# Scores of both heads of an early pair issued in turns into two PSUM banks, in one step

## The chip, the cores and the metric

The kernel runs on one core of a Trainium2 chip. The metric is the device time of one execution in microseconds, taken over several runs. The trace is that of one profiled execution, and its times count from the start of its span.

## The reference

An attention with a memory, then two feed-forward layers over all 2304 tokens. B = 4 batches, H = 8 heads, S = 576 tokens, D = 64; the model's width is 512, the inner width of the layers 2048.

```python
scores = scale * np.matmul(q, k.transpose(0, 1, 3, 2))        # per head 576 x 576, causal
a = exp(scores - rowmax); a /= a.sum(-1) + 1e-09
local = np.matmul(a, v)
q_p = phi(q)                                                  # elu(q) + 1
mem_out = (q_p @ M_prev) / (q_p @ z_prev + 1e-6)
attn = g * mem_out + (1 - g) * local                          # g = sigmoid(beta) per head
x = attn, heads side by side: 2304 x 512
h = x @ w_in;  g = max(h, 0) + log1p(exp(-|h|));  x = g @ w_out
h = x @ w_in2; g = h if h > 0 else exp(h) - 1;    out = g @ w_out2
```

## The kernel before

**Staging.** Each batch's attention is cut into part A, the first 256 tokens (two query tiles, 0 and 1, of 128 rows), and part B, the other 320. The layers run over five chunks of tokens: chunk 0 is part A of batches 0 and 1, chunk 1 part A of batches 2 and 3, and chunks 2 to 4 hold the parts B. So the parts A of batches 0 and 1 come first, at the start of the program (`chain`), and every other attention part is side work: `sides()` is a generator that is advanced while a chunk's layer runs. The layer's loop (`ffn`) has 16 f steps of 12 matmuls (L572 to L574, four k of three each, into a bank "h"), an activation (L548 to L551 in layer 0: Abs, Exp, Ln, then a DVE step), a cast and a difference (L576, L577), and then 16 output steps of 12 matmuls (L588 to L590). All products are in full precision from two or three passes of a split operand; a plain fp32 matmul shows as two records in the trace.

**What sets the order.** `TUNE["order"]` lists chunk and layer with shares: (1.9, 0.0) says that 1.9 steps of side work and 0.0 weight conversions are owed for every f step, and the second bracket says so for every output step. `conv` says after which step of the start the conversion of weights begins, and in what rhythm. Within that, a scheduler orders the instructions of each engine by priority and by its own estimate of times; so an instruction's place in the program text is not its place in an engine's queue. Each engine works through its queue in order.

**Part A in the plain path.** A pair p is two heads; head h of a pair lies in partitions 64h to 64h + 63. One score matmul multiplies 128 query columns of one head by 128 (tile 0) or 256 (tile 1) key columns, over 64 rows of the array (`product`, L294). `bank(n)` gives a 2 KB bank from "h" (four buffers, shared with the layers) for batches 0 and 1, and from pss (three buffers, shared with the transposes "tp") for batches 2 and 3. `scores(n, (0, 1))` writes tile 0 of one head into a bank, lets DVE reduce it with the mask into `sph` and `neg` (L320), lets ACT take exp (L326), and then does tile 1 in the same bank. `normalise` scales the rows of sph, `group` transposes them (L361) and copies them to `pt`, `gather_pair` multiplies with v and the memory (L392, L395), and an ACT cast and a DVE difference write the layer's operand x (L142, L143). `feature(p)` computes phi and its norm: ACT L241 and L242 (reading `ar`, loaded by POOL at L192 to L198), DVE L243 to L252; `feature_t` transposes it (L261).

Early in the program PE's order has, among others, one behind the other: h_553 of 128 columns (an odd head), h_426 of 256 columns (an odd head), h_590 of 128 columns (an even head).

**Weights.** `convert` builds the two-part weights (L506, L508, L97) and stores them to DRAM scratch; SP loads them again for later chunks (L532).

Of the kernel before, what the change touches and what calls it, by code (L numbers as in the profile page):

```python
# [10 lines left out]
ACTF = mybir.ActivationFunctionType  # L11
ALU = mybir.AluOpType
AX = mybir.AxisListType
I32 = mybir.dt.int32
# [21 lines left out]
WIDTH = [sum(n for _, _, n in c) for c in CHUNKS]  # L36
SLOT = (0, 1, 2, 0, 1)
TUNE = dict(
    st='q', pri=(200, 200), conv=(4, 2, 14), inw=4, ahead=(3, 3, 0), pads=0, plain=(0, 1, 2, 3),
    hi='ssss ssss', lo='v', sc='vv vvv ssv', pt='s ssv', eva='sv',  # L40


    order=((0, 0, (1.9, 0.0), (0.8, 0.2)), (1, 0, (0.2, 0.2), (0.8, 0.6)), (0, 1, (1.1, 0.0), (1.2, 0.0)), (1, 1, (1.1, 0.0), (1.5, 0.0)), (2, 0, (0.4, 0.0), (1.2, 0.0)), (2, 1, (0.8, 0.0), (1.2, 0.0)), (3, 0, (0.4, 0.0), (1.2, 0.0)), (3, 1, (0.8, 0.0), (1.0, 0.0)), (4, 0, (0.0, 0.0), (0.0, 0.0)), (4, 1, (0.0, 0.0), (0.0, 0.0))),
)


# [12 lines left out]
def kernel(  # L59
# [85 lines left out]
    def attention(b, part, pool, early=None):  # L145
# [159 lines left out]
        def scores(n, todo):  # L305
            P = sph[n % 2]
            neg = d["neg", n]
            ps = None
            for i in todo:
                w_ = width(i)  # L310
                pieces = ((0, w_),) if i < 4 else ((0, S // 2), (S // 2, S // 2))
                for k, (k0, kn) in enumerate(pieces):
                    if first:
                        ps = ps if i else bank(n)
                        s = ps[:, poff(0, i):poff(0, i) + kn]
                    else:
                        s = bank(0)[:, :kn]
                    product(n, i, s, k0, kn)
                    mk0 = 512 - 128 * i + k0
                    ve.tensor_tensor_reduce(  # L320
                        out=P[:, poff(n, i) + k0:poff(n, i) + k0 + kn], in0=s, in1=mask[:, mk0:mk0 + kn],
                        scale=-0.125, scalar=3.0e38 if k == 0 else neg[:, 5:6], op0=ALU.add, op1=ALU.min,
                        accum_out=neg[:, 5:6] if i == 4 and k == 0 else neg[:, i:i + 1],
                    )
                Pi = P[:, poff(n, i):poff(n, i) + w_]
                se.activation(Pi, Pi, ACTF.Exp, scale=-1.0, bias=neg[:, i:i + 1], accum_out=sums(n, i))  # L326

        def scale(n):
            P = sph[n % 2]
# [90 lines left out]
        feature(0)  # L420
        prep_v(0)
        yield
        for n in range(H):
            p, hh = divmod(n, 2)
            start(n)
            if not plain and n + 1 < H:
                prep_qk(n + 1)
            if first:
                if hh == 0:
                    feature_t(p)  # L430
                scores(n, (0, 1))
                if hh and p + 2 < NP:
                    load_kq(p + 2)
                yield
                normalise(n)
                if hh == 0 and n:
                    group(n - 2, d["pt", n - 2][0], ((1, 0), (0, 0), (1, 1)))
                    group(n - 1, d["pt", n - 1][0], ((1, 0), (0, 0), (1, 1)))
                    yield
                    gather_pair(n - 2)  # L440
                    if p + 2 < NP:
                        load_rest(p + 2)
                if hh == 0 and p + 1 < NP:
                    feature(p + 1)
                d["pt", n] = targets(n)
                if n + 1 < H:
                    prep_v(n + 1)
                yield
                continue
            scores(n, (2,))  # L450
            yield
            if n:
# [46 lines left out]
    def convert(src, key, w=None):  # L499
        wr = tri.tile([128, 4, 128], F32, name="wr", tag="wr")  # L500
        if wide:
            w64 = tri.tile([128, 4, 128, 2], I32, name="w64", tag="big")
            nc.sync.dma_start(w64.rearrange("p k n t -> p (k n t)"), src.bitcast(I32))
            low, high = w64[:, :, :, 0], w64[:, :, :, 1]
            wi = wr.bitcast(I32)
            se.activation(wr, high.bitcast(F32), ACTF.Prelu, scale=2.0 ** -112, alpha=-(2.0 ** 32))  # L506
            ve.tensor_scalar(wi, wi, 3, None, ALU.logical_shift_left)
            ve.scalar_tensor_tensor(wi, low, 29, wi, ALU.logical_shift_right, ALU.bitwise_or)  # L508
        else:
            nc.sync.dma_start(wr.rearrange("p k n -> p (k n)"), src)  # L510
        if w is None:
            w = w64.rearrange("p k n t -> p (k n t)").rearrange("p (s k n) -> p s k n", s=2, k=4).bitcast(F32R)
        hi, lo = w[:, 0], w[:, 1]
        copy(E[T["hi"].split()["o" in key][int(key[0])]], hi, wr)
        E[T["lo"]].tensor_sub(lo, wr, f32(hi))
        scratch[key] = dram.tile([128, 2, 4, 128], F32, name=f"s_{key}", tag=f"s_{key}")
        E[T['st']].dma_start(scratch[key], f32(w))
# [109 lines left out]
    def chain(parts, ahead):  # L627

        parts, active = list(parts), []
        while parts or active:  # L630
            if parts and (not active or len(active) == 1 and active[0][2] <= ahead):
                b, part, pool, early = parts.pop(0)
                active.append([(b, part), attention(b, part, pool, early), 21 if part == "A" else 43])
            for a in list(active):
                a[2] -= 1
                if next(a[1], a) is a:
# [118 lines left out]
```

## Time and profile before

| | |
|---|---|
| time, median of 3 runs | 1084.99 us (1078.2 to 1086.96) |
| profiled execution: span | 1077.9 us |
| profiled execution: own time | the page gives no time beside the span |
| PE busy | 1043.4 us, 97% of the span |
| DVE busy, ACT busy | 684.7 us (64%), 670.5 us (62%) |
| POOL busy | 90.5 us (8%) |
| DMA moved | 251.65 MB, 233 GB/s |

PE is TensorE, DVE VectorE, ACT ScalarE, POOL GpSimd, SP SyncE; PEld is the loading of weights into TensorE. A row of the timeline gives a start, a duration, the engine, the line, what is written and read, and in brackets the idle time ahead with what ended it. Matmuls overlap, so the time that one takes of PE is the distance to the next one's start, not its duration. PEclk is the granted clock as a share of 2.4 GHz.

### The profile page before, as it was taken

To read this page: it belongs to the slowest core of one execution; us is meant where nothing else is said; L and a number is where in the kernel's file an instruction comes from. 1 tells how busy PE (TensorE), PEld (TensorE's weight loads), DVE (VectorE), ACT (ScalarE), POOL (GpSimd) and SP (SyncE) were. 2 spreads that over 40 slices of the span, in tenths; PEclk is the share of its full clock that TensorE was granted. 3 is DMA by queue.
4 is the path that set the end of the run, shared out by engine and by line. 5 is a ranking of instruction groups with operands and counts; after the bars stand their busy time and mean duration, and the time that the engine had idled before them with its cause. 6 is when DMAs were issued, how large, how long until landed. Compare 5 with 4: busy or idle time off the path is not lost.

```text
span 1077.9 us, 15779 instructions
## 1 busy us (share of the span) xinstructions
PE 1043.4 (97%) x5328; PEld 906.1 (84%) x5328; DVE 684.7 (64%) x1698; ACT 670.5 (62%) x1458; POOL 90.5 (8%) x173
## 2 busy tenths in 40 slices
PE   6799999989999999999999999999999999999998
PEld 3456676667888888888889998999999999999998
DVE  6966787666567998798557756875575271150540
ACT  5858886588558987576659945654796251480330
POOL 5222331000000000000000000000000000000000
PEclk9789999989999999999999999999999999999999
DMA  8891588887875788755765655666655477877775
GB/s 264 312 332 50 185 288 299 291 303 283 293 273 204 248 277 302 277 197 164 231 219 192 219 201 194 225 225 204 219 176 173 159 254 247 253 233 234 230 234 175
DMA packets 73120, 251.65 MB, mean 233 GB/s; under 512 B 10320, under 2 KB 14928, under 8 KB 73040
## 3 DMA queue, kind: packets, MB, share of 16 engines
q1 hardware_dynamic: 64432, 216.56, 59.2%
q0 software_dynamic: 8608, 34.09, 10.1%
q8 instruction: 42, 0.69, 0.3%
q14 instruction: 38, 0.31, 0.1%
HBM read 212.34 MB, written 38.27 MB: 233 GB/s over the span
## 4 chain that ended last, share of the span: by engine, by line
PE 82%; DMA 7%; DVE 5%; ACT 3%; issue 1%; SPq 0%; POOL 0%; DVEq 0%; ACTq 0%
PE h L588 12%; PE h L589 12%; PE h L590 12%; PE h L572 11%; PE h L573 10%; PE h L574 10%; PE tp L361 5%; DMA s_1i<-w 3%; PE o L376 2%; DMA w<-in_w2i 2%; PE s L298 2%; DMA w<-in_w1i 2%; PE h L298 1%; PE s L294 1%; PE o L377 1%
## 5 line engine op out<-in xcount | busy, mean ns | idle before, releaser
L572 PE MATMUL h<-x,w 128*128 128x512 f32 (+2 forms) x640 | 238.8, 379 | 10.7 <-ACT x L142 3.8
L573 PE MATMUL h<-x,w 128*128 128x512 f32 (+2 forms) x640 | 240.2, 375 | 0.0
L574 PE MATMUL h<-x,w 128*128 128x512 f32 (+2 forms) x640 | 240.1, 375 | 0.0
L588 PE MATMUL h<-g,w 128*128 128x512 f32 (+2 forms) x640 | 238.2, 373 | 0.2 <-DVE neg L320 0.2
L589 PE MATMUL h<-g,w 128*128 128x512 f32 (+2 forms) x640 | 237.2, 371 | 0.0
L590 PE MATMUL h<-g,w 128*128 128x512 f32 (+2 forms) x640 | 237.0, 371 | 0.0
L572 PEld LDWEIGHTS h<-x,w 128*128 128x128 f32 x640 | 120.7, 189 | 27.7 <-ACT x L142 4.5
L573 PEld LDWEIGHTS h<-x,w 128*128 128x128 f32 x640 | 121.4, 190 | 13.4 <-issue 1.5
L574 PEld LDWEIGHTS h<-x,w 128*128 128x128 f32 x640 | 121.4, 190 | 13.4 <-issue 0.3
L588 PEld LDWEIGHTS h<-g,w 128*128 128x128 f32 x640 | 120.2, 188 | 12.9 <-issue 0.7
L590 PEld LDWEIGHTS h<-g,w 128*128 128x128 f32 x640 | 120.2, 188 | 12.1 <-issue 1.0
L589 PEld LDWEIGHTS h<-g,w 128*128 128x128 f32 x640 | 120.3, 188 | 11.8 <-DVE sph L336 0.4
L577 DVE TENSOR_TENSOR g<-t,g 128x512 fp32r<-128x512 f32 (+2 forms) x160 | 100.9, 634 | 34.1 <-ACT g L576 32.7
L326 ACT ACTIVATE sph<-sph,neg 128x576 f32<-128x576 f32 (+2 forms) x160 | 96.2, 602 | 38.3 <-DVE neg L320 37.8
L576 ACT CAST g<-t 128x512 fp32r<-128x512 f32 (+2 forms) x160 | 91.3, 573 | 23.5 <-DVE t L559 19.2
L551 DVE SCALAR_TENSOR_TENSOR t<-h,t 128x512 f32<-128x512 f32 (+2 forms) x80 | 50.7, 636 | 61.2 <-ACT t L550 60.8
L367 DVE TENSOR_TENSOR ptb<-tp,ptb 128x512 fp32r<-128x512 f32 (+2 forms) x96 | 53.3, 575 | 39.0 <-ACT ptb L366 38.7
L320 DVE CUSTOM_DVE_ANT_0 sph<-s,mask 128x128 f32<-128x128 f32 (+4 forms) x80 | 38.4, 483 | 59.6 <-PE s L298 37.6
L366 ACT CAST ptb<-tp 128x512 fp32r<-128x512 f32 (+2 forms) x96 | 45.0, 498 | 47.6 <-PE tp L361 47.1
L361 PE MATMUL tp<-ident,sph 128*128 128x128 f32 x480 | 71.6, 282 | 0.4 <-DVE sph L336 0.4
L361 PEld LDWEIGHTS tp<-ident,sph 128*128 128x128 f32 x480 | 60.3, 146 | 7.7 <-DVE sph L336 1.0
L506 ACT ACTIVATE wr<-w 128x512 f32<-128x512 f32 x64 | 42.7, 667 | 33.0 <-DMA w<-in_w2i 14.1
(112 smaller groups left out, 1517.9 us busy)
## 6 DMA issues: line engine op xcount, KB each, us to landing
w<-s_1i SPq DMA_DIRECT2D x79, 512.0 KB, 3.8
w<-s_0i SPq DMA_DIRECT2D x64, 512.0 KB, 4.3
w<-s_0o SPq DMA_DIRECT2D x64, 512.0 KB, 3.9
w<-s_1o SPq DMA_DIRECT2D x64, 512.0 KB, 4.2
qk<-in_qk POOLq DMA_DIRECT2D x32, 480.0 KB, 5.0
w<-in_w1i SPq DMA_DIRECT2D x16, 512.0 KB, 5.7
s_0i<-w SPq DMA_DIRECT2D x16, 512.0 KB, 5.6
w<-in_w1o SPq DMA_DIRECT2D x16, 512.0 KB, 4.7
```

The costliest lines, as they stand in the source:

```text
L326: se.activation(Pi, Pi, ACTF.Exp, scale=-1.0, bias=neg[:, i:i + 1], accum_out=sums(n, i))
L361: te.transpose(pt[:, c:c + 128], P[:, poff(n, i) + 128 * j:poff(n, i) + 128 * j + 128], ident)
L367: ve.tensor_sub(dst[:, 1, :c], pt[:, :c], f32(dst)[:, 0, :c])
L551: ve.scalar_tensor_tensor(t, h, 0.0, t, ALU.max, ALU.add)
L572: te.matmul(h[:, :N], hi[:, k, :], xk[:, 0, :N], start=k == 0, stop=False)
L573: te.matmul(h[:, :N], hi[:, k, :], xk[:, 1, :N], start=False, stop=False)
L574: te.matmul(h[:, :N], lo[:, k, :], xk[:, 0, :N], start=False, stop=k == KD - 1)
L576: se.copy(g[:, 0, :N], t[:, :N])
L577: ve.tensor_sub(g[:, 1, :N], t[:, :N], f32(g)[:, 0, :N])
L588: te.matmul(h[:, :N], hi[:, k, :], gs[f][:, 0, :N], start=f == 0, stop=False)
L589: te.matmul(h[:, :N], hi[:, k, :], gs[f][:, 1, :N], start=False, stop=False)
L590: te.matmul(h[:, :N], lo[:, k, :], gs[f][:, 0, :N], start=False, stop=f == KF - 1)
```

## The change

One generator step now treats both heads of a pair. `scores_pair(n)` takes two banks, one for each head, issues tile 1 of both heads and then tile 0 of both heads, and then, head by head, the DVE reduction and the ACT exp of tile 1 and of tile 0. The loop over heads becomes a loop over pairs for the parts A. A part A takes 17 steps in place of 21. The shares of chunk 0, layer 0, are lowered from 1.9 and 0.8 to 1.6 and 0.6, and the first conversion comes after step 3 in place of 4. The w64 tile is also allocated where weights aren't wide.

```diff
--- before.py
+++ after.py
@@ -36,11 +36,11 @@
 WIDTH = [sum(n for _, _, n in c) for c in CHUNKS]
 SLOT = (0, 1, 2, 0, 1)
 TUNE = dict(
-    st='q', pri=(200, 200), conv=(4, 2, 14), inw=4, ahead=(3, 3, 0), pads=0, plain=(0, 1, 2, 3),
+    st='q', pri=(200, 200), conv=(3, 2, 14), inw=4, ahead=(3, 3, 0), pads=0, plain=(0, 1, 2, 3),
     hi='ssss ssss', lo='v', sc='vv vvv ssv', pt='s ssv', eva='sv',
 
 
-    order=((0, 0, (1.9, 0.0), (0.8, 0.2)), (1, 0, (0.2, 0.2), (0.8, 0.6)), (0, 1, (1.1, 0.0), (1.2, 0.0)), (1, 1, (1.1, 0.0), (1.5, 0.0)), (2, 0, (0.4, 0.0), (1.2, 0.0)), (2, 1, (0.8, 0.0), (1.2, 0.0)), (3, 0, (0.4, 0.0), (1.2, 0.0)), (3, 1, (0.8, 0.0), (1.0, 0.0)), (4, 0, (0.0, 0.0), (0.0, 0.0)), (4, 1, (0.0, 0.0), (0.0, 0.0))),
+    order=((0, 0, (1.6, 0.0), (0.6, 0.2)), (1, 0, (0.2, 0.2), (0.8, 0.6)), (0, 1, (1.1, 0.0), (1.2, 0.0)), (1, 1, (1.1, 0.0), (1.5, 0.0)), (2, 0, (0.4, 0.0), (1.2, 0.0)), (2, 1, (0.8, 0.0), (1.2, 0.0)), (3, 0, (0.4, 0.0), (1.2, 0.0)), (3, 1, (0.8, 0.0), (1.0, 0.0)), (4, 0, (0.0, 0.0), (0.0, 0.0)), (4, 1, (0.0, 0.0), (0.0, 0.0))),
 )
 
 
@@ -305,16 +305,11 @@
         def scores(n, todo):
             P = sph[n % 2]
             neg = d["neg", n]
-            ps = None
             for i in todo:
                 w_ = width(i)
                 pieces = ((0, w_),) if i < 4 else ((0, S // 2), (S // 2, S // 2))
                 for k, (k0, kn) in enumerate(pieces):
-                    if first:
-                        ps = ps if i else bank(n)
-                        s = ps[:, poff(0, i):poff(0, i) + kn]
-                    else:
-                        s = bank(0)[:, :kn]
+                    s = bank(0)[:, :kn]
                     product(n, i, s, k0, kn)
                     mk0 = 512 - 128 * i + k0
                     ve.tensor_tensor_reduce(
@@ -324,6 +319,23 @@
                     )
                 Pi = P[:, poff(n, i):poff(n, i) + w_]
                 se.activation(Pi, Pi, ACTF.Exp, scale=-1.0, bias=neg[:, i:i + 1], accum_out=sums(n, i))
+
+        def scores_pair(n):
+            ps = [bank(n), bank(n + 1)]
+            for i in (1, 0):
+                w_, at = width(i), poff(0, i)
+                for h in range(2):
+                    product(n + h, i, ps[h][:, at:at + w_], 0, w_)
+            for h in range(2):
+                P, neg = sph[h], d["neg", n + h]
+                for i in (1, 0):
+                    w_, at, to = width(i), poff(0, i), poff(n, i)
+                    ve.tensor_tensor_reduce(
+                        out=P[:, to:to + w_], in0=ps[h][:, at:at + w_], in1=mask[:, 512 - 128 * i:512 - 128 * i + w_],
+                        scale=-0.125, scalar=3.0e38, op0=ALU.add, op1=ALU.min, accum_out=neg[:, i:i + 1],
+                    )
+                    Pi = P[:, to:to + w_]
+                    se.activation(Pi, Pi, ACTF.Exp, scale=-1.0, bias=neg[:, i:i + 1], accum_out=sums(n + h, i))
 
         def scale(n):
             P = sph[n % 2]
@@ -420,33 +432,36 @@
         feature(0)
         prep_v(0)
         yield
-        for n in range(H):
+        for p in range(NP if first else 0):
+            n = 2 * p
+            start(n)
+            start(n + 1)
+            feature_t(p)
+            scores_pair(n)
+            if p + 2 < NP:
+                load_kq(p + 2)
+            yield
+            if p:
+                group(n - 2, d["pt", n - 2][0], ((1, 0), (0, 0), (1, 1)))
+                group(n - 1, d["pt", n - 1][0], ((1, 0), (0, 0), (1, 1)))
+                yield
+                gather_pair(n - 2)
+                if p + 2 < NP:
+                    load_rest(p + 2)
+            if p + 1 < NP:
+                feature(p + 1)
+            yield
+            normalise(n + 1)
+            for m in (n, n + 1):
+                d["pt", m] = targets(m)
+                if m + 1 < H:
+                    prep_v(m + 1)
+            yield
+        for n in range(0 if first else H):
             p, hh = divmod(n, 2)
             start(n)
             if not plain and n + 1 < H:
                 prep_qk(n + 1)
-            if first:
...
             scores(n, (2,))
             yield
             if n:
@@ -507,6 +522,7 @@
             ve.tensor_scalar(wi, wi, 3, None, ALU.logical_shift_left)
             ve.scalar_tensor_tensor(wi, low, 29, wi, ALU.logical_shift_right, ALU.bitwise_or)
         else:
+            w64 = tri.tile([128, 4, 128, 2], I32, name="w64", tag="big")
             nc.sync.dma_start(wr.rearrange("p k n -> p (k n)"), src)
         if w is None:
             w = w64.rearrange("p k n t -> p (k n t)").rearrange("p (s k n) -> p s k n", s=2, k=4).bitcast(F32R)
@@ -630,7 +646,7 @@
         while parts or active:
             if parts and (not active or len(active) == 1 and active[0][2] <= ahead):
                 b, part, pool, early = parts.pop(0)
-                active.append([(b, part), attention(b, part, pool, early), 21 if part == "A" else 43])
+                active.append([(b, part), attention(b, part, pool, early), 17 if part == "A" else 43])
             for a in list(active):
                 a[2] -= 1
                 if next(a[1], a) is a:
```

Inserted lines shift the numbers: L320, L548 to L551, L572 and L588 to L590 of before are L333, L564 to L567, L588 and L604 to L606 of the change; L392 and L395 are L404 and L407.

PE's queue at the first pair of batch 2 (s_908 and s_948, then s_909 and s_910, are the two heads' score banks; h is a layer bank). Before:

```order
L294 MATMUL s_908<-kq_845 128x128 [waits DMASW3_49,DMASW2_49]
L294 MATMUL s_948<-kq_845 128x128 [waits DMASW5_49,DMASW4_49]
L261 MATMUL tp_990<-ident_89,e_915 128x128 [waits DVE_49,Activation_49]
...
L572 MATMUL h_1115<-x0_0_96,w_404 128x512 [waits DVE_49]
...
L574 MATMUL h_1115<-x0_3_99,w_404 128x512
L294 MATMUL s_908<-kq_845 128x256 [waits DVE_49]
L294 MATMUL s_948<-kq_845 128x256 [waits DVE_49]
L572 MATMUL h_1166<-x0_0_96,w_433 128x512 [waits DVE_49]
```

And now:

```order
L261 MATMUL tp_904<-ident_89,e_870 128x128
L294 MATMUL s_909<-kq_845 128x256 [waits DMASW3_49,DMASW2_49]
L294 MATMUL s_910<-kq_845 128x256 [waits DMASW5_49,DMASW4_49,PE_49]
L294 MATMUL s_909<-kq_845 128x128
L294 MATMUL s_910<-kq_845 128x128
L588 MATMUL h_1123<-x0_0_96,w_456 128x512 [waits DVE_49]
L589 MATMUL h_1123<-x0_0_96,w_456 128x512
```

The two matmuls of a head, which stood 18 rows apart with a wait for DVE ahead of the second, now follow each other, in turns with those of the other head.

ACT's queue at the first layer's first two f steps (t_821 and t_880 are their activations, x0_3 the last operand of chunk 0, e and ar belong to `feature` of batch 2's first pairs). Before:

```order
L142 CAST x0_3_99<-o_803 128x256 [waits PE_49]
L548 ACTIVATE t_821<-h_823 128x512 [waits PE_49]
L548 ACTIVATE t_880<-h_882 128x512 [waits PE_49]
L549 ACTIVATE t_821<-t_821 128x512 [waits Activation_49]
L549 ACTIVATE t_880<-t_880 128x512 [waits Activation_49]
L550 ACTIVATE t_821<-t_821,ones_91 128x512 [waits Activation_49]
L241 ACTIVATE e_870<-ar_850 128x256 [waits DMASW4_49,DMASW6_49,DMASW3_49,DMASW7_49,DMASW2_49,DMASW0_49]
...
L550 ACTIVATE t_880<-t_880,ones_91 128x512 [waits Activation_49]
L242 ACTIVATE ar_850<-ar_850,ones_91 128x256 [waits Activation_49]
```

And now:

```order
L142 CAST x0_3_99<-o_803 128x256 [waits PE_49]
L564 ACTIVATE t_821<-h_823 128x512 [waits PE_49]
L241 ACTIVATE e_870<-ar_850 128x256 [waits DMASW4_49,DMASW3_49,DMASW6_49,DMASW2_49,DMASW7_49,DMASW0_49,Activation_49]
L241 ACTIVATE e_928<-ar_860 128x256 [waits DMASW2_49]
L564 ACTIVATE t_880<-h_882 128x512 [waits PE_49]
L565 ACTIVATE t_821<-t_821 128x512 [waits Activation_49]
L242 ACTIVATE ar_850<-ar_850,ones_91 128x256 [waits Activation_49]
L242 ACTIVATE ar_860<-ar_860,ones_91 128x256 [waits DMASW7_49,DMASW0_49,Activation_49]
L565 ACTIVATE t_880<-t_880 128x512 [waits Activation_49]
```

The two L241 moved ahead of the second f's first activation, and the two L242 ahead of its second.

PE's queue where chunk 1 begins (x1_2 and x1_3 are operands of chunk 1, o_2135 is the last gather of batch 3, g and h_2012 belong to chunk 0's output steps). Before:

```order
L574 MATMUL h_2255<-x1_1_101,w_2251 128x512
L572 MATMUL h_2186<-x1_2_102,w_2182 128x512 [waits Activation_49]
L572 MATMUL h_2209<-x1_2_102,w_2205 128x512
L572 MATMUL h_2232<-x1_2_102,w_2228 128x512
...
L392 MATMUL o_2135<-phi_1895,ar_1571 64x256 [waits DVE_49]
L392 MATMUL o_2135<-phi_1895,ar_1571 64x256
L573 MATMUL h_2186<-x1_2_102,w_2182 128x512
...
L395 MATMUL o_2135<-pt_2066,ar_1571 64x128
L572 MATMUL h_2186<-x1_3_103,w_2182 128x512 [waits Activation_49]
L572 MATMUL h_2209<-x1_3_103,w_2205 128x512
```

And now:

```order
L404 MATMUL o_2135<-phi_1872,ar_1552 64x256 [waits DMASW5_49,DVE_49]
L404 MATMUL o_2135<-phi_1872,ar_1552 64x256
L407 MATMUL o_2135<-pt_2042,ar_1552 64x256 [waits DMASW4_49,Activation_49]
...
L407 MATMUL o_2135<-pt_2043,ar_1552 64x128
L606 MATMUL h_2012<-g_1122,w_2044 128x512
L604 MATMUL h_2012<-g_1172,w_2044 128x512
...
L606 MATMUL h_2012<-g_1579,w_2110 128x512
L385 MATMUL o_2800<-phi_2568,ms_2176 128x320 [waits DVE_49]
L588 MATMUL h_2186<-x1_0_100,w_2182 128x512 [waits DMAHW1_49]
L589 MATMUL h_2186<-x1_0_100,w_2182 128x512
...
L588 MATMUL h_2186<-x1_3_103,w_2182 128x512 [waits Activation_49]
```

Before, all of chunk 0's output matmuls were through, and four f steps of chunk 1 were begun operand by operand ahead of the last gather; now 28 output matmuls stand behind that gather, and chunk 1's f steps follow whole.

## Rows read from the trace of the kernel before

**Rows 1.** The page, part 1: busy time, share of the span, instructions.
```profile
PE 1043.4 (97%) x5328; PEld 906.1 (84%) x5328; DVE 684.7 (64%) x1698; ACT 670.5 (62%) x1458; POOL 90.5 (8%) x173
```

**Rows 2.** Busy time by window: PE, PEld, DVE, ACT, POOL, granted clock, DMA share, GB/s.
```profile
40.00:60.00 20.00, 16.56 (x67) 10.42 (x68) 19.55 (x70) 15.89 (x43) 4.04 (x8) 0.59 0.96 349
80.00:100.00 20.00, 17.82 (x76) 12.75 (x74) 12.73 (x38) 16.46 (x39) 7.29 (x14) 0.91 0.24 68
100.00:120.00 20.00, 20.00 (x89) 13.61 (x89) 13.31 (x46) 17.06 (x40) 4.43 (x8) 1.00 0.21 65
200.00:220.00 20.00, 17.58 (x86) 11.41 (x86) 15.29 (x46) 12.39 (x33) 2.20 (x5) 1.00 0.66 225
220.00:240.00 20.00, 17.22 (x64) 13.35 (x63) 13.54 (x26) 16.86 (x31) 1.07 (x2) 0.83 0.89 313
```

**Rows 3.** PE's waits, 0 to 300 us: total, times, longest.
```profile
PE h L572 <- ACT x L142: 3.8, 3, 2.1
...
PE h L294 <- DVE neg L320: 0.3, 1, 0.3
```

**Rows 4.** Timeline of PE, 96 to 114 us: start, duration, instruction.
```profile
96.07 0.39 PE L573 MATMUL h<-x,w 128*128 128x512 f32 x1
96.30 0.39 PE L574 MATMUL h<-x,w 128*128 128x512 f32 x1
96.62 0.70 PE L294 MATMUL s<-kq 64*128 64x256 f32 x4
97.25 0.50 PE L572 MATMUL h<-x,w 128*128 128x512 f32 x1
97.59 0.39 PE L573 MATMUL h<-x,w 128*128 128x512 f32 x1
...
107.85 0.48 PE L294 MATMUL s<-kq 64*128 64x128 f32 x2
108.26 0.65 PE L395 MATMUL o<-pt,ar 128*64 128x256 f32 x2
...
113.17 0.70 PE L294 MATMUL s<-kq 64*128 64x256 f32 x2
113.80 0.50 PE L574 MATMUL h<-x,w 128*128 128x512 f32 x1
```

**Rows 5.** Timeline of PE, what ran between 21.81 and 22.04 us.
```profile
21.80 0.59 PE L294 MATMUL h<-kq 64*128 64x128 f32 x2
```

**Rows 6.** Timeline of PE at the second chunk's start.
```profile
219.53 1.19 PE L572 MATMUL h<-x,w 128*128 128x512 f32 x4 [2.15 <-ACT x L142]
...
226.78 0.47 PE L572 MATMUL h<-x,w 128*128 128x512 f32 x1 [2.78 <-DVE g L577]
```

**Rows 7.** Timeline of all engines, 77 to 86 us, down to e's first steps.
```profile
79.34 0.71 POOL L194 DMA_DIRECT2D ar<-in_vm  x1
...
81.22 1.09 ACT L548 ACTIVATE t<-h 128x512 f32<-128x512 f32 x2 [3.07 <-PE h L574]
...
82.19 1.15 ACT L549 ACTIVATE t<-t 128x512 f32<-128x512 f32 x2
...
83.23 0.72 ACT L550 ACTIVATE t<-t,ones 128x512 f32<-128x512 f32 x1
83.84 0.72 ACT L241 ACTIVATE e<-ar 128x256 f32<-128x256 f32 x2
...
83.98 0.69 DVE L551 SCALAR_TENSOR_TENSOR t<-h,t 128x512 f32<-128x512 f32 x1 [5.38 <-ACT t L550]
...
84.73 0.79 PE L572 MATMUL h<-x,w 128*128 128x512 f32 x1 [2.14 <-DVE t L551]
...
85.07 0.90 ACT L242 ACTIVATE ar<-ar,ones 128x256 f32<-128x256 f32 x2
...
85.81 0.75 DVE L243 SCALAR_TENSOR_TENSOR e<-e,ar 128x256 f32<-128x256 f32 x2
```

**Rows 8.** Tile ar, 60 to 215 us: time from a load's issue to landing.
```profile
DMA to landing us min/median/max: 2.1/3.4/6.8
```

More of the change, by code (lines that the diff above doesn't have):

```diff
@@ L427, in attention @@
                 prep_qk(n + 1)
-            if first:
[L429 to L449, printed above, removed]
             scores(n, (2,))
```

## The prediction

> **What bounds the kernel now.** The page's first part comes first: PE is busy 97% of the span [rows 1], so time leaves the span only if PE gets less to do or waits less. The second view, the busy time of 20 us windows [rows 2], says where PE waits. At 100 to 120 it is busy 20.00 of 20.00, and so in the four windows to 200; at 80 to 100, 200 to 220 and 220 to 240 it is busy 17.82, 17.58 and 17.22, and in two of these the granted clock is 0.91 and 0.83. A clock of 0.83 over 20 us is 6.8 us at 1.2 GHz in place of 2.4, so 3.4 us lost; 0.91 loses 1.8. At 40 to 60 another engine sets the pace: DVE 19.55, PE 16.56, clock 0.59. The third view, PE's waits by releaser [rows 3], and the timeline at the longest of them [rows 6, 7] name what ends last: ACT's cast of x (L142), DVE's last step of g (L577), DVE's softplus (L551). The wait that the change takes away, a score matmul waiting for DVE's reduction (L320) of the same bank, cost PE 0.3 us, once. So the wait itself is worth almost nothing. The gain, if any, is in PE's slots for scores and in what the new order does to the three stalls. Behind PE's row of about 1030 (around 300 us) the two programs run the same PE order, so I count nothing there.
>
> **Part 1: score slots, 88 to 212 us.** Here PE is the bound, so each slot counts. A slot is the time from one start to the next [rows 4]. Of batches 2 and 3 there are 8 pairs, so 32 matmuls. A lone 128-wide takes 108.26 − 107.85 = 0.41, a lone 256-wide 113.80 − 113.17 = 0.63. So 128 columns more cost 0.22, and 0.41 − 0.22 = 0.19 is paid once for a run. The FFN matmul ahead of a run and the one behind it take 0.32 and 0.34 in place of 0.23: 0.20 more for a run that stands between FFN matmuls. Two heads' 256-wide together (x4) also take 0.63: the second half is free.
> Before, the timeline has 29 separate runs: 13 of one 128-wide, 13 of one 256-wide, three in which both heads sit together (the rows shown, by pattern). That is 13 × 0.41 + 13 × 0.63 + 1.8 = 15.3, and about 5.1 for the sides (29 × 0.20 = 5.8, less where a run's neighbour is no FFN matmul). Sum 20.4.
> After, the order has 16 runs: 3 with a whole pair, 7 with both matmuls of one head, 6 with one matmul. The scheduler keeps the turns in three pairs only. One head's 256 and 128 back to back is 0.63 + 0.22 = 0.85; a whole pair is 0.85 as well if the halves overlap. 10 × 0.85 + 3 × 0.63 + 3 × 0.41 = 11.6, sides 16 × 0.20 less neighbours, 3.0. Sum 14.6. **−5.8 us.** Bounds: 0 if each run pays drains that no row shows, −10 if all pairs ran as one run without sides. I take the row-by-row sum.
> One of the whole-pair runs issues A256 A128 B256 B128, so it depends on whether B may start while A's second still waits. The trace has a run like that at 21.8: in PE's order a 128-wide of an odd head, a 256-wide of an odd head, then a 128-wide of an even head, which sits in the other half. By 22.04 the two 128-wides have both started, and no 256-wide [rows 5].
> The Trainium skill, "PSUM — Partial Sum Buffer", in its passage on the engines' queues, says that MATMULs start and complete in program order. By that, B's 256 would wait until A's 128 has started, the run would take about 0.4 us more, and part 1 would be −5.4. The row speaks for the overlap, and the two sums differ by too little to show in the time.
>
> **Part 2: the start of the second chunk, 209 to 231 us.** Before, PE runs out of the first chunk's output matmuls before the last pair of batch 3 is through; it takes k = 0 to 2 of four f steps early, then waits 2.15 us for the cast of x1_3 and 2.78 for g [rows 6], and loses the 3.4 us to the clock. 8.3 in all. After, the last gather of batch 3 stands in PE's order ahead of 28 output matmuls (28 × 0.23 = 6.4 us of work), and only then comes chunk 1, whole f by whole f. So the cast gets 6.4 us of cover where it needed 2.15; ACT's softplus of f0 then starts after 12 matmuls, not after 44. What may spoil it: in ACT's queue a cast of R, which waits for qk's load, now stands right ahead of that cast. Bounds 0 and −8.3. I take three quarters, **−6.3**, as the cover is three times the wait but a first f of a chunk always has its own latency.
>
> **Part 3: the first FFN block, 77 to 88 us.** PE stops at 84.73 − 2.14 = 82.6 because the bank of f0 is freed by DVE at 84.7. Before, ACT does f0, f1 (L548), both L549, one L550, and only then e of the two next pairs [rows 7]. After, e_870 and e_928 and their L242 stand between. e_870 waits for ar loads, the last of which POOL issues at 79.34; such loads land 3.4 us after issue, 2.1 to 6.8 [rows 8]. So ACT is held from 81.8, when f0's L548 ends, to about 82.7; then e twice 0.72, L548 0.55, L549 0.57, L242 twice 0.90, L549 0.57, L550 0.72: 86.8, then DVE 0.69, 87.5 in place of 84.7, so +2.8. DVE's five feature steps ahead of its softplus (two L243 0.75, three more of about 0.4) run while ACT is at L549 and L550. With 0.2 for a somewhat longer stretch at the lower clock: **+3.0**; bounds 0 (PE comes later itself, so that the release is not late for it) and +7.9 (the third rival).
>
> **Part 4: the start, up to 63 us.** DVE is the bound there. It has the same reductions and conversions, but about 1.1 us less work stands ahead of the steps that free the first FFN matmul. PE's half-clock work is beside it. **−1.0**; bounds −3.4 and +3.4, PE's idle time in 40 to 60 (20 − 16.56). The dropped bank wait is worth 0.3 at most [rows 3]; the kq loads, released up to a step later or earlier, are issued long before use. The changed table of shares, the chain's length of 17 steps and the w64 tile add no instruction.
>
> **Sum**: −5.8 − 6.3 + 3.0 − 1.0 = −10.1. The profiled execution has a span of 1077.9, 0.3 below the lowest of the three runs and 7.1 below their median; the sum is made on its stalls, and carried over as a difference: 1067.8 there, **1074.9** on the median of 1084.99.
>
> **Rivals.** (1) *The stall moves.* In 200 to 240 us the DMA engines are busy 0.66 and 0.89 of the time [rows 2]; if transfers of weights, not the order, set when chunk 1 can run, part 2 gives nothing: −5.8 + 3.0 − 1.0 = −3.8, 1081. For it: chunk 1's f steps wait for a weight load each in PE's order. Against: the two waits there end with ACT and DVE, none with a DMA.
> (2) *The change does not do what it says.* The turns are kept in 3 of 16 pairs; if also the merged runs cost what the split ones do, part 1 is 0: −4.3, 1080.7. Against: x4 in 0.63.
> (3) *Slower: ACT is held by a load ahead of the softplus.* Place: e_870 in ACT's queue at 82 us. Price: if its load lands at the slow end, 79.34 + 6.8 = 86.1, the same 4.0 of ACT work and 0.69 of DVE free the bank at 90.9, 6.1 later than before, and the longer stop costs once more what the clock costs at 80 to 100 now, 1.8: +7.9. ACT carries the delay on to the cast of x1_3, so that the slots of part 1 are only waited away and part 2 is 0: with part 4, +6.9, 1091.9. It decides once the load lands more than 1 us behind my 82.7 and ACT has not caught up by 209. For it: ACT was held there by nothing before and is now held by a load. Against: the median landing.
>
> **Numbers.** Chances: forecast 0.62, its own range 1068 to 1081 (parts 2 and 3 by half either way); rival 1 0.18, rival 2 0.07, rival 3 0.13. Range 1064 to 1092: upwards it takes in the rivals up to the price of the third, downwards the full part 2 with part 3 at 0 and some of part 4's bound. What a measurement of this kernel can tell from no change is about 1%, 10.8 us. The forecast lies just inside it. As the bounds of its parts reach further down (−21.7 if all were at their ends) than up (+11.3), I split its chance 0.38 faster and 0.24 the same. Rivals 1 and 2 are the same, and so is 0.03 of rival 3, whose price stays inside the bound if only the first e is held; the other 0.10 is slower, where the same place in ACT's queue holds the e of later pairs too. Faster 0.38, the same 0.52, slower 0.10.
>
> **What would show it.** Part 1: scores in 88 to 212 in 16 runs, a pair of one head 0.85. Part 2: the windows 200 to 240 with over 19 of 20 busy and a clock of 1.00. Part 3: PE's wait for the softplus at the first block about 5, in place of 2.1. Part 4: first FFN matmul at about 62. The prediction is wrong if the 209 to 231 stall is still there, if ACT stands at e for more than 3 us, or if stalls appear between 100 and 200, where there were none.

## The result, and the profile after

| | before | change |
|---|---|---|
| median | 1084.51 us, 4 runs (1078.2 to 1086.96) | 1069.13 us, 4 runs (1067.87 to 1071.51) |
| ratio to before, 95% interval | | 0.9886 [0.9862, 0.991] |
| span of the profiled execution | 1077.9 us | 1068.4 us |

The change is 1.14% faster, 12.4 us by the ratio; the two profiled executions differ by 9.5 us. The two medians above lie further apart, 15.4 us: the four runs of the kernel before spread over 8.8 us, and in its later runs, beside the experiments, its medians were 1080.4 to 1081.4 us, which puts 1069.13 at 0.989 to 0.990, as the ratio does. The forecast was 1074.9, in a range of 1064 to 1092; it is a ratio of 0.991, and −10.1 us as a difference of profiles.

Three points in time can be read in both traces: the first matmul of the layers, the fifth f step (the first that needs a freed bank), and the 701st layer matmul, near 300 us, from where the difference only wanders between −9.1 and −10.1.

| stage | before | change | difference |
|---|---|---|---|
| to the first layer matmul | 63.20 us | 65.63 us | +2.4 |
| from there to the fifth f step | 21.53 | 23.03 | +1.5 |
| from there to the 701st layer matmul | 218.69, of them PE idle 8.01 | 204.85, idle 1.97 | −13.8 |

So the change loses 3.9 us ahead of the place where it wins 13.8. Busy time of the change by window (PE, PEld, DVE, ACT, POOL, granted clock, DMA share, GB/s); it answers to [rows 2]:

```profile
20.00:40.00 20.00, 7.83 (x36) 4.56 (x35) 15.44 (x52) 12.37 (x34) 5.75 (x11) 0.75 0.85 280
40.00:60.00 20.00, 14.60 (x79) 9.20 (x78) 19.85 (x77) 17.58 (x53) 4.15 (x8) 0.76 0.97 347
80.00:100.00 20.00, 16.24 (x63) 12.56 (x62) 10.08 (x30) 14.06 (x28) 8.19 (x15) 0.83 0.22 60
100.00:120.00 20.00, 20.00 (x102) 14.91 (x102) 15.96 (x57) 19.36 (x54) 7.31 (x14) 1.00 0.21 55
200.00:220.00 20.00, 19.14 (x88) 14.58 (x88) 13.49 (x27) 11.54 (x21) 1.57 (x4) 1.00 0.97 375
220.00:240.00 20.00, 20.00 (x88) 16.29 (x87) 14.22 (x26) 19.48 (x37) 0.54 (x1) 1.00 0.95 338
```

At 200 to 240 PE is now busy 19.14 and 20.00 of 20, with the clock at 1.00 throughout. At 80 to 100 it is less busy than before, 16.24, and at 20 to 40 it stands for more than half the time. PE's waits of the change, 0 to 300 us (total, times, longest), which answer to [rows 3]:

```profile
PE tp L261 <- DVE e L252: 9.5, 2, 8.2
...
PE h L588 <- DVE t L567: 3.8, 1, 3.8
PE tp L261 <- DVE nrm L249: 3.2, 1, 3.2
...
PE h L588 <- ACT x L142: 1.3, 2, 0.9
...
PE h L588 <- DMA w<-s_0i: 0.9, 2, 0.6
```

The wait for g (2.8) is gone, that for the casts of x is 1.3 in place of 3.8. New is a wait of 8.2 us for e at the start, and the wait at the fifth f step is 3.8 where it was 2.1.

The timeline of PE at score runs of the change, which answers to [rows 4]:

```profile
97.48 0.92 PE L294 MATMUL s<-kq 64*128 64x256 f32 x8
98.33 0.50 PE L588 MATMUL h<-x,w 128*128 128x512 f32 x1
...
103.23 0.93 PE L294 MATMUL s<-kq 64*128 64x256 f32 x8
104.09 0.50 PE L589 MATMUL h<-x,w 128*128 128x512 f32 x1
```

A run of four score matmuls, both heads, takes 98.33 − 97.48 = 0.85 us where it is issued in turns. At 103.23 it is issued head by head (256, 128, 256, 128) and takes 0.86. Runs of one head take 0.85, those of one matmul 0.63 and 0.41 or 0.42, as before. There are 16 runs, and the sum of their slots is 11.6 us (forecast 11.6); before it was 15.4.

The timeline of PE where chunk 1 begins, which answers to [rows 6]:

```profile
207.69 0.40 PE L606 MATMUL h<-g,w 128*128 128x512 f32 x1
...
208.07 0.39 PE L588 MATMUL h<-x,w 128*128 128x512 f32 x1
...
211.29 0.50 PE L588 MATMUL h<-x,w 128*128 128x512 f32 x1 [0.27 <-DMA w<-s_0i]
...
214.94 0.50 PE L588 MATMUL h<-x,w 128*128 128x512 f32 x1 [0.60 <-DMA w<-s_0i]
```

The output matmuls of chunk 0 run up to 207.9, chunk 1 follows without a stop, and the waits left are 0.27 and 0.60 us, for weight loads. Before they were 2.15 and 2.78, and the slots behind them were 0.43 in place of 0.23.

The timeline of all engines at the first f steps of the change, which answers to [rows 7]:

```profile
83.55 0.60 ACT L564 ACTIVATE t<-h 128x512 f32<-128x512 f32 x1 [3.08 <-PE h L590]
...
84.04 0.71 ACT L241 ACTIVATE e<-ar 128x256 f32<-128x256 f32 x2
...
84.66 0.59 ACT L564 ACTIVATE t<-h 128x512 f32<-128x512 f32 x1
...
85.13 0.63 ACT L565 ACTIVATE t<-t 128x512 f32<-128x512 f32 x1
...
85.65 0.90 ACT L242 ACTIVATE ar<-ar,ones 128x256 f32<-128x256 f32 x2
...
86.19 0.82 DVE L243 SCALAR_TENSOR_TENSOR e<-e,ar 128x256 f32<-128x256 f32 x2 [5.26 <-DMA ar<-in_vm]
...
86.45 0.62 ACT L565 ACTIVATE t<-t 128x512 f32<-128x512 f32 x1
...
86.97 1.32 ACT L566 ACTIVATE t<-t,ones 128x512 f32<-128x512 f32 x2
...
87.93 0.68 DVE L567 SCALAR_TENSOR_TENSOR t<-h,t 128x512 f32<-128x512 f32 x1
...
88.66 0.79 PE L588 MATMUL h<-x,w 128*128 128x512 f32 x1 [3.76 <-DVE t L567]
```

ACT does both e (L241) at 84.04, without a wait: the loads had landed. It then does f1's L564, f0's L565, both L242, f1's L565 and both L566. DVE's first step of `feature` needs the first L242, which ACT does at 85.65; the 5.26 us of idle time ahead of it are put down to a load, but the load that e needs (L192, issued at 80.6) had landed 2.4 us after its issue. DVE has five steps of `feature` between 86.19 and 87.93. So the softplus of f0 is ready at 88.6, and PE stands for 3.76 us. After that its slots are 0.43 up to 94.8; before that lasted to 87.9.

### The profile page after: what moved, and what is told of

Read it like the earlier page. It is cut to its first block, busy times and chain, and to the rows that moved or that the text cites. A ratio compares the mean times of both kernels' runs of the same rounds, so it can differ in the third digit from the quotient of the medians.

```text
span 1068.4 us, 15784 instructions
## 1 busy us (share of the span) xinstructions
PE 1029.8 (96%) x5328; PEld 904.2 (85%) x5328; DVE 683.7 (64%) x1698; ACT 669.3 (63%) x1458; POOL 90.7 (8%) x173
## 3 DMA queue, kind: packets, MB, share of 16 engines
q0 software_dynamic: 8608, 34.09, 10.4%
## 4 chain that ended last, share of the span: by engine, by line
PE 85%; DMA 5%; DVE 3%; ACT 1%; issue 1%; POOL 0%; SPq 0%; ACTq 0%; DVEq 0%; POOLq 0%
PE h L588 12%; PE h L604 12%; PE h L606 11%; PE h L605 11%; PE h L589 11%; PE h L590 11%; PE tp L373 4%; PE o L388 2%; PE s L298 2%; PE h L298 1%; PE o L407 1%; PE o L389 1%; DMA s_1i<-w 1%; PE s L294 1%; DMA w<-s_0i 1%
## 5 line engine op out<-in xcount | busy, mean ns | idle before, releaser
L588 PE MATMUL h<-x,w 128*128 128x512 f32 (+2 forms) x640 | 239.1, 378 | 7.7 <-DVE t L567 3.8
L590 PE MATMUL h<-x,w 128*128 128x512 f32 (+2 forms) x640 | 239.4, 374 | 0.0
L604 PE MATMUL h<-g,w 128*128 128x512 f32 (+2 forms) x640 | 238.0, 373 | 1.0 <-DMA w<-s_0o 0.8
L606 PE MATMUL h<-g,w 128*128 128x512 f32 (+2 forms) x640 | 237.3, 372 | 0.0
L588 PEld LDWEIGHTS h<-x,w 128*128 128x128 f32 x640 | 120.8, 189 | 23.1 <-DVE t L567 4.2
L590 PEld LDWEIGHTS h<-x,w 128*128 128x128 f32 x640 | 121.0, 189 | 12.9
L604 PEld LDWEIGHTS h<-g,w 128*128 128x128 f32 x640 | 120.2, 188 | 13.7 <-DMA w<-s_0o 1.2
L606 PEld LDWEIGHTS h<-g,w 128*128 128x128 f32 x640 | 120.2, 188 | 12.2 <-issue 1.3
L321 ACT ACTIVATE sph<-sph,neg 128x384 f32<-128x384 f32 (+2 forms) x96 | 67.5, 703 | 32.0 <-DVE neg L315 31.4
L567 DVE SCALAR_TENSOR_TENSOR t<-h,t 128x512 f32<-128x512 f32 (+2 forms) x80 | 50.8, 635 | 54.4 <-ACT t L566 54.0
L521 ACT ACTIVATE wr<-w 128x512 f32<-128x512 f32 x64 | 42.7, 669 | 32.1 <-DMA w<-in_w2i 12.1
L574 ACT ACTIVATE t<-t 128x416 f32<-128x416 f32 (+2 forms) x64 | 36.8, 579 | 40.7 <-DVE t L573 37.3
```

The costliest lines, as they stand in the source:

```text
L567: ve.scalar_tensor_tensor(t, h, 0.0, t, ALU.max, ALU.add)
L588: te.matmul(h[:, :N], hi[:, k, :], xk[:, 0, :N], start=k == 0, stop=False)
L590: te.matmul(h[:, :N], lo[:, k, :], xk[:, 0, :N], start=False, stop=k == KD - 1)
L604: te.matmul(h[:, :N], hi[:, k, :], gs[f][:, 0, :N], start=f == 0, stop=False)
L606: te.matmul(h[:, :N], lo[:, k, :], gs[f][:, 0, :N], start=False, stop=f == KF - 1)
```

## The experiments

"Ratio" is that of each kernel's runs to the kernel before's on the same chip. Stages are those of the table above, "slots" the sum of the score runs' slots behind the fifth f step, "idle" PE's idle time from there to the 701st layer matmul.

| kernel | ratio [95%] | first layer matmul | to fifth f | score runs, slots | idle |
|---|---|---|---|---|---|
| before | 1 | 63.2 | 21.5 | 29, 15.4 | 8.0 |
| the change | 0.9886 [0.9862, 0.991] | 65.6 | 23.0 | 16, 11.6 | 2.0 |
| table_only | 1.0016 [0.9999, 1.0034] | 63.0 | 21.5 | 30, 15.8 | 12.1 |
| early_pairs_only | 1.0092 [1.0068, 1.0115] | 65.2 | 23.0 | 29, 15.2 | 13.7 |
| late_pairs_only | 0.982 [0.9786, 0.9854] | 62.7 | 21.5 | 12, 9.6 | 5.2 |
| late_pairs_old_shares | 0.9814 [0.9789, 0.9839] | 62.7 | 21.5 | 12, 9.6 | 3.9 |
| head_step_one_bank | 0.9933 [0.9906, 0.996] | 65.2 | 24.5 | 17, 13.1 | 2.5 |
| late_head_step | 0.984 [0.9815, 0.9866] | 61.6 | 21.5 | 15, 13.0 | 2.8 |
| pair_without_turns | 0.9876 [0.9844, 0.9909] | 66.4 | 23.0 | 14, 11.2 | 3.5 |
| late_pairs_no_turns | 0.9822 [0.9782, 0.9861] | 62.6 | 21.5 | 13, 10.4 | 4.8 |
| side_earlier | 0.9999 [0.9979, 1.0019] | 62.8 | 21.5 | 29, 18.5 | 7.0 |
| conversion_later | 0.9898 [0.987, 0.9926] | 66.4 | 23.0 | 16, 11.6 | 1.9 |
| e_behind_softplus | 0.9955 [0.9937, 0.9973] | 66.9 | 21.5 | 14, 11.2 | 4.4 |
| late_pairs_e_behind | 0.9858 [0.9834, 0.9882] | 63.0 | 21.6 | 12, 10.2 | 1.2 |

**The numbers alone.** The edit is the two lines of TUNE in the diff, nothing else.

> Only the changed numbers: shares 1.6 and 0.6 for chunk 0's first layer, first conversion after step 3; attention as before. Theory A (the gain comes from the merged score runs of batches 2 and 3 and the order that follows from them): nothing, -1 to +1 us, first FFN matmul at 63.2 +- 0.5, the waits of 2.1 and 2.8 us at 219 and 226 us still there. Rival B (the lower shares alone calm the side work and remove the stall at chunk 1): -6 to -8 us and those waits gone.

Measured 1.0016, and the stall is there, if in other pieces. PE's waits of it from 200 us:

```profile
PE h L572 <- DMA w<-s_0i: 3.6, 1, 3.6
PE o L395 <- ACT pt L97: 2.2, 1, 2.2
PE h L572 <- ACT x L142: 2.2, 1, 2.2
```

The new shares and the earlier conversion carry none of the gain. In the profiled execution, the slowest of the ten, they made the stall longer (idle 12.1). Rival B falls.

**The early and the late pairs apart.** `late_pairs_only` keeps the loop over heads for batches 0 and 1, `early_pairs_only` for batches 2 and 3; both have the first conversion after step 3:

```diff
-        for p in range(NP if first else 0):
+        for p in range(NP if first and b > 1 else 0):     # late_pairs_only; b < 2 in early_pairs_only
...
-        for n in range(0 if first else H):
+        for n in range(0 if first and b > 1 else H):      # with the loop of before for the others
```

> The paired step for batches 2 and 3 alone, with the new table; batches 0 and 1 keep the per-head loop. Theory A: the loss at the start (+2.4 us at the first FFN matmul) goes, the merged runs and the chunk 1 order stay: -2.4 us against the full change, so a ratio to the kernel before near 0.986. Rival C (the early pairs' new order is what lets the later side work run ahead): no better than half of the change's gain, ratio 0.994 or more.

> The paired step for batches 0 and 1 alone, old shares, batches 2 and 3 per head. Theory A: first FFN matmul at 65.6, score runs of batches 2 and 3 still 29 with slots of 15.4 us in sum, stall at chunk 1 still there: +2 to +3 us, ratio near 1.002. Rival C: -5 us or more.

The paired step gains 1.8% where it stands behind the start, and loses 0.9% where it stands in it. The sign of each was expected; the sizes were −2.4 us for the late pairs against the change and +2 to +3 for the early ones, and the ratios make them about −7 and +10. Rival C falls in both. The early pairs' order costs more than its 2 us at the first layer matmul: it also comes with the longer stop at the fifth f step, and everything arrives later at chunk 1. PE's waits of `early_pairs_only`, 60 to 303 us:

```profile
PE h L615 <- DVE t L594: 5.2, 2, 3.8
PE h L615 <- ACT x L142: 3.6, 4, 1.8
PE h L615 <- DMA w<-s_0i: 3.5, 1, 3.5
PE tp L378 <- DVE sph L353: 2.6, 1, 2.6
```

The 3.8 us at the fifth f step (the longest of the first row) and the stall at chunk 1 (most of the others) stand side by side there. In the full change, with the merged runs of the late pairs, that stall doesn't come: PE's idle time is 2.0 us where it is 13.7 here.

**The old shares with the late pairs.** Only the shares 1.9 and 0.8 are put back.

> The paired step for batches 2 and 3 alone, with the shares 1.9 and 0.8 of before and the first conversion after step 3. Side work then comes earlier still. Theory A: the stall at chunk 1 stays away, scores' slots near 9.6; the time within 2 us of late_pairs_only (ratio 0.980 to 0.984). Rival B (the lower shares carry part of the gain): ratio 0.987 or more, with PE waiting for ACT or DVE in the f loop between 90 and 160 us.

0.9814 against 0.982: the same within the intervals, and the lowest median of all, 1061.8 us. With the paired step in place these runs show no difference between the two sets of shares.

**Merging a head's matmuls, without a second head or a second bank.** `head_step_one_bank` issues tile 1 and tile 0 of one head ahead of its two reductions; `late_head_step` does so for batches 2 and 3 alone.

```diff
-            ps = None
-            for i in todo:
+            if first:                                     # late_head_step: first and b > 1
+                ps = bank(n)
+                for i in (1, 0):
+                    product(n, i, ps[:, poff(0, i):poff(0, i) + width(i)], 0, width(i))
+            for i in ((1, 0) if first else todo):
```

> As before, head by head and one bank for each head, but both score matmuls of a head (256-wide, then 128-wide) are issued ahead of the two reductions; old shares. Theory A: most of the slots are won without a second bank or turns: 17 runs, scores' slots near 12 us in place of 15.4, in all -5 to -9 us. Rival D (two heads in two banks are needed): scores' slots stay near 15.4 and the time within 2 us of before.

> As before with the numbers of before, but for batches 2 and 3 both score matmuls of a head are issued ahead of its two reductions, still head by head in one bank. It parts the merging of a head's two matmuls from the step for two heads. Theory A: first FFN matmul at 63, 15 runs, scores' slots 12 to 13 us, the stall at chunk 1 mostly gone: -8 to -11 us, ratio near 0.991; the step for two heads is then worth the 4 to 8 us that are left to late_pairs_only. Rival H (merging is all): ratio 0.982 to 0.985 as with the late pairs.

The runs are 17 and 15, as theory A had them, and the slots 13.1 and 13.0 (near 12, and 12 to 13). `head_step_one_bank` lands in theory A's time. But `late_head_step` is at 0.984, where rival H had it: it has nearly the whole gain of the late pairs. The timeline of PE at its first score runs:

```profile
95.51 0.92 PE L294 MATMUL s<-kq 64*128 64x256 f32 x4
96.36 0.50 PE L578 MATMUL h<-x,w 128*128 128x512 f32 x1
...
99.99 0.92 PE L294 MATMUL s<-kq 64*128 64x256 f32 x4
100.83 0.50 PE L578 MATMUL h<-x,w 128*128 128x512 f32 x1
```

One head's two matmuls in one bank take 0.85 us, as in the change. Two heads that share a run save 3.4 us more of slots (13.0 against 9.6); in the time 0.982 [0.9786, 0.9854] against 0.984 [0.9815, 0.9866] is no difference that these runs can tell. What counts is that no DVE reduction stands between a head's two matmuls; what the second bank and the second head add is too little to show.

**The turns.** The loop over heads is put outside that over tiles, in the change (`pair_without_turns`) and in the late pairs with old shares (`late_pairs_no_turns`):

```diff
-            for i in (1, 0):
-                w_, at = width(i), poff(0, i)
-                for h in range(2):
+            for h in range(2):
+                for i in (1, 0):
+                    w_, at = width(i), poff(0, i)
                     product(n + h, i, ps[h][:, at:at + w_], 0, w_)
```

> The full change, but scores_pair issues both matmuls of the first head, then both of the second, each in its own bank. By the rows at 21.8 us a later matmul of the other half starts ahead of an earlier one: a run of four takes 0.85 here as well, and the ratio is that of the change, 0.988 +- 0.003. Rival F (matmuls strictly in program order): a run of four takes 1.24 or more, some +3 us over all late pairs.

> late_pairs_old_shares with the first head's two matmuls ahead of the second's, each in its own bank. If the turns are worth nothing: scores' slots 9.5 to 10.5, ratio 0.981 +- 0.003. If turns matter once all pairs are together: slots over 11 and ratio 0.984 or more.

0.9876 and 0.9822: the same as with turns. Rival F falls, and the change's own trace says why. What ran on PE between 103.2 and 103.26 us, in the run that is issued as 256, 128, 256, 128:

```profile
103.23 0.49 PE L294 MATMUL s<-kq 64*128 64x256 f32 x2
```

A matmul has two records, but those of one 256-wide start 0.32 us apart. The kernel before shows it where a 256-wide runs alone; what ran on PE there between 113.1 and 113.4 us:

```profile
113.17 0.48 PE L294 MATMUL s<-kq 64*128 64x256 f32 x1
```

So the two records by 103.26 are the first ones of two 256-wide matmuls: both have started, though the first head's 128-wide stands between them in the queue. The Trainium skill, "PSUM — Partial Sum Buffer", section "Engine vs sequencer instructions", says that MATMULs start and complete in program order. The row at 103.23 disagrees for two matmuls in different halves of the rows, and such a run takes 0.86 us against 0.85 in turns. The measurement decides.

**The stall as a matter of order alone.** The kernel before with shares of 2.3 and 0.9.

> The kernel before with higher shares alone (2.3 and 0.9 in place of 1.9 and 0.8), so that the side work of batches 2 and 3 comes earlier and the last gather stands ahead of a good part of chunk 0's output matmuls; score runs stay 29, one bank for a head, wait between the two matmuls. Theory A (part 2 is a matter of order): the waits of 2.1 and 2.8 us at chunk 1 and the two half-clock stretches go, -5 to -8 us, scores' slots stay at 15.4. Rival E (the stall goes only if the scores themselves get shorter; hurried side work makes the f loop wait elsewhere): within 2 us of before, or slower.

0.9999: rival E. The waits of 2.1 and 2.8 us at chunk 1 went, and others came. PE's waits from 84 to 303 us:

```profile
PE tp L361 <- DVE sph L336: 2.2, 2, 1.4
PE h L572 <- DVE t L551: 2.1, 1, 2.1
PE h L298 <- DVE R L220: 1.2, 1, 1.2
PE h L572 <- DMA w<-s_0i: 1.0, 1, 1.0
PE o L395 <- ACT pt L97: 0.9, 1, 0.9
```

The stop at the fifth f step is the 2.1 of the second row, the wait for a weight load (1.0) comes at 250.9 us; the rest is spread over 183 to 215 us. The idle time is 7.0 in place of 8.0, and the score slots with the waits in them grew to 18.5. Side work that is only hurried meets its own chain through DVE and ACT sooner. So the order that leaves the output matmuls as cover did not pay here without the merged runs; that they make it pay by shortening the chain behind it is argued, not shown by itself.

**The start.** `conversion_later` puts the first conversion of the change back behind step 4.

> The full change with the first weight conversion after step 4, as before, in place of 3. If the earlier conversions cause the 2.4 us lost at the start (DVE waits 3.0 us for ACT's wr there): first FFN matmul at 63.2 to 64, time -2 us against the change, ratio 0.986. Rival G (the paired order of the early pairs causes it): first FFN matmul at 65.6 +- 0.5, ratio 0.988 to 0.991.

Rival G: 66.4, not 63.2. This point differs by more than a microsecond even between kernels whose early pairs are the same. In the eight kernels of the table whose early pairs are those of before it is 61.6 to 63.2, in the six others 65.2 to 66.9. One of these six is `head_step_one_bank` (65.2), which has neither the step for a pair, nor the second bank, nor the earlier conversion. So what costs here is the merged order of the early pairs, and the change's own trace shows how. All engines, 32 to 40 us:

```profile
32.42 0.40 DVE L246 TENSOR_REDUCE nrm<-ar 128x4 f32<-128x256 f32 x1
...
35.15 0.66 ACT L521 ACTIVATE wr<-w 128x512 f32<-128x512 f32 x1 [4.45 <-DMA w<-in_w1i]
...
35.84 0.43 DVE L522 TENSOR_SCALAR wr<-wr 128x512 int32<-128x512 int32 x1 [3.02 <-ACT wr L521]
...
39.04 0.42 DVE L252 TENSOR_TENSOR e<-e,nrm 128x256 f32<-128x256 f32 x1
...
39.52 0.69 PE L261 MATMUL tp<-ident,e 128*128 128x128 f32 x2 [8.19 <-DVE e L252]
```

DVE stops at 32.8, because the head of its queue is a conversion whose ACT step (L521) waited 4.45 us for a weight load. The last step of e for the third pair (L252, at 39.04) stands behind it, and PE waits 8.19 us for that e. In DVE's queue of the change six conversions stand ahead of the third pair's e with their first two steps, four of them whole; in that of before it is three, none of them whole, and in `conversion_later` the same six. `late_pairs_only` has the start of before; its wait for e, 0 to 64 us:

```profile
PE tp L261 <- DVE e L252: 1.4, 1, 1.4
```

That the conversions ahead of e are the cause, and not another part of the early pairs' order, is read from the traces; it wasn't tried by itself, since a later first conversion leaves these six where they are in the queue.

**The first f steps.** Here e of batch 2's first two pairs takes a zero bias from a column that ACT writes behind the second f's activation, in the change (`e_behind_softplus`) and in the late pairs (`late_pairs_e_behind`):

```diff
+            if (c, layer, f) == (0, 0, 1):
+                se.activation(zero[0], t[:, :1], ACTF.Identity, scale=0.0)
...
-        owed = due = 0.0
+        owed, due = -3.2 if (c, layer) == (0, 0) else 0.0, 0.0      # -3.8 with the late pairs
...
+                se.activation(e, q, ACTF.Exp, bias=zero[0])         # b == 2 and p < 2
```

> The full change, but e of batch 2's first two pairs takes its bias (zero) from a column that ACT writes behind the activation of the second f step, so that ACT and DVE do both softplus first; the side work starts two f steps later. Part 3: PE's wait at the fifth f falls from 3.8 to 2.2 or less and the stretch at the lower clock gets shorter: -1.5 to -3 us against the change, ratio 0.985 to 0.988. Rival: the later side work gives it back at chunk 1 (waits there over 1.5 us), ratio 0.988 or more.

> late_pairs_old_shares with e of batch 2's first two pairs behind the second f step's softplus, as in e_behind_softplus: an attempt at a version better than both. PE's wait at the fifth f falls from 2.2 to about 1.6; side work starts later, which the shares of 1.9 have to make up: ratio 0.979 to 0.983. If the later start leaves waits at chunk 1, 0.984 or more.

PE's matmul of the fifth f step in `e_behind_softplus`:

```profile
88.40 0.49 PE L593 MATMUL h<-x,w 128*128 128x512 f32 x1 [2.15 <-DVE t L572]
```

The wait fell from 3.76 to 2.15, so the queue order on ACT and DVE was its cause. But the time rose, to 0.9955, where the rival had it. The side work starts later, and at chunk 1 PE waits 2.4 us for g again. That is only a part: of the 6.5 us between the two profiled executions 3.1 arise from the fifth f step to the 701st layer matmul, 1.3 at the start, and 3.7 behind that matmul, where PE's idle time is no longer than in the change; 1.6 are won ahead of the fifth f step. With the late pairs the idle time up to 300 us is the lowest of all, 1.2, and still the ratio is 0.9858, no better than without (0.9814). There too it isn't waiting: PE's idle time over the whole span is 2.2 us less, its busy time 5.0 us more (1035.6 against 1030.6). Where in the slots this arises, and why, isn't settled. No version of these beats the late pairs with the old numbers.

## Why the prediction was right, and where it was not

The sum was −10.1 and the profiles differ by −9.5. Its parts, with what the traces give for each:

| part | forecast | measured | how |
|---|---|---|---|
| 1 score runs | −5.8 | −6.6 | slots 15.4 to 11.6; 2.8 of the matmuls around them |
| 2 chunk 1 | −6.3 | −6.9 | waits 5.2 to 0.9; 13 slots at 0.43 gone, 0.2 each |
| 3 first f steps | +3.0 | +2.9 | 1.5 to the fifth f; seven more slots at 0.43 |
| 4 start | −1.0 | +2.4 | first layer matmul 63.20 to 65.63 |
| about 250 to 300 us | 0 | −1.7 | waits 2.8 to 1.1 |

The 2.8 in the first row is what is left of the 7.8 us by which PE's busy time fell behind the fifth f step, after 3.8 of slots and 1.2 for the clock (13 slots less in part 2, seven more in part 3). It is a remainder, not a reading: about 0.8 of it are in the slots of layer matmuls, the rest in those of the transposes and gathers.

That the sum is off by only 0.6 us is luck in part. The start came out 3.4 us worse than forecast, and the gains in parts 1 and 2 and in a stretch that was put at nothing (−1.7) were larger by about as much.

- **Part 1** was right in number and in cause: 16 runs, 0.85 for a pair or for one head, and the overlap of the halves without turns. The sides, forecast at −2.1, are within the −2.8. The rival by program order does not hold.
- **Part 2** was right in size. Its reason, that it is "a matter of order", was half of it: `side_earlier` has much of the order without the merged runs and gains nothing. Parts 1 and 2 are not two independent terms. The cost of the lower clock there was put at 3.4 us from the mean clock of the window; 13 slots at 0.43 make 2.6.
- **Part 3** was right in mechanism, the queue of ACT and DVE. That the size came out as well is luck. The wait was to grow by 2.8 us and grew by 1.6 (2.14 to 3.76), the lower clock was to cost 0.2 and cost 1.4. In the forecast ACT stood until 82.7 for a load issued at 79.34; but e reads only q, which the first of a pair's four loads brings (L192, issued at 78.3 before; at 80.6 in the change, landed 2.4 us later), so e never waited. For the same reason rival 3 did not come about.
- **Part 4** is the step that failed, in its sign. It counted 1.1 us less of DVE's work ahead of the first layer matmul, and not what that work waits for. By that matmul DVE was in fact busy 1.5 us longer (52.28 against 50.75) and idle 0.9 longer (13.35 against 12.45); its waits for ACT's step of a conversion grew from 1.9 to 5.1 us, those for score matmuls fell from 5.0 to 1.8. In this start a conversion that stands earlier in DVE's queue held all that is behind it until its weights had landed. The bounds of ±3.4 took it in.
- The part behind 300 us was right to be left out: the difference between the two traces moves by 1.0 us at most there, and by 0.4 from its start to the end.

Rival 1 (weight transfers set when chunk 1 can run) did not come about in the change, where they end 0.27 and 0.60 us of waits. It isn't empty, though: in `table_only` and `early_pairs_only` the longest wait at chunk 1 is for a weight load, 3.6 and 3.5 us. In `side_earlier` the stall moved as well, but to waits for DVE and ACT. Rival 2 was half true, since the turns are kept in three pairs only; it cost nothing, as the turns do nothing here.

## What to carry to other kernels

Where a product goes through the same bank in two pieces with a reduction between them, issue both pieces first: here that alone, for the pairs behind the start, gave 0.984 in one bank and without a second head. Try such a change stage by stage, for what helps where PE is the bound (0.982) can cost at a start where DVE and the loads set the pace (1.0092; DVE busy 19.85 of 20 us, the DMA engines 0.97 at 40 to 60 us), and one number for the whole hides both. And when counting the work that stands ahead of something in an in-order queue, count what each instruction waits for too.

## What the runs showed of the hardware that was not expected

- A matmul in one half of the rows overtook one of the other half that stood ahead of it in PE's queue (103.23 us, above), so PE's queue is not strictly in order there. The order inside a run of half-height matmuls changed nothing that could be measured, 0.86 against 0.85 us.
- A run of half-height matmuls costs more than its slots: with the FFN matmul ahead of and behind it [rows 4] 0.20 us each time it is entered and left. For the 13 runs that went this would be 2.6 us if each stood between FFN matmuls. The layer matmuls next to score runs did give back 1.8 us, but those next to other matmuls of the attention took 0.9 more.
- After a stop of 3.76 us in the change the lower of the two clock levels stayed for 6.1 us (slots of 0.43, 88.66 to 94.8), after one of 2.14 us before for 3.2 us (84.73 to 87.9). So the same queue order was paid twice: in the stop, and in the longer stretch at 1.2 GHz.
